# A new task order for the first chunk of an attention + softplus FFN kernel, and ten start-up products in place of eight

## The chip, the cores and the metric

The kernel runs on one core of one Trainium2 chip. The metric is the device time of one execution in microseconds, as the median of several runs. The core has five engines that run side by side, each working through its own queue strictly in order: TensorE (PE, matrix products; its weight loads are shown apart as PEld), VectorE (DVE), ScalarE (ACT), GpSimd (POOL), and SyncE (SP), which here only issues transfers between HBM and the on-chip memory. An instruction that has to wait holds up everything behind it in its own queue.

## The reference, cut to what matters

```python
# q, k, v: (8 batches, 8 heads, 576 positions, 64)
scores = scale * np.matmul(q, k.transpose(0, 1, 3, 2))
# heads 0-3: only the last 32 positions; heads 4-7: every 32nd position back
scores = np.where(masks[None, :, :, :], scores, -1000000000.0)
scores = scores - np.max(scores, axis=-1, keepdims=True)
attn = np.exp(scores)
attn = attn / (np.sum(attn, axis=-1, keepdims=True) + 1e-09)
x = np.matmul(attn, v)          # then laid out as (4608 tokens, 512)
h = x @ w_in                    # 512 -> 2048
g = np.maximum(h, 0.0) + np.log1p(np.exp(-np.abs(h)))
out = g @ w_out                 # 2048 -> 512
```

The weights arrive as float64 and all products are made from a high and a low part, so that the result keeps float32 accuracy: each of `x @ w_in` and `g @ w_out` is three products (high·high, high·low, low·high).

## The kernel before

**Tiling.** The 4608 tokens are cut into 9 chunks of 512. The hidden width of 2048 is cut into 16 slices `f` of 128. For each chunk and slice, `hidden` (L638) makes 12 products of 128x128 by 128x512 on TensorE (task `F`), `log_part` runs three activations on ScalarE (`A`, `Ae`, `Al`), `softplus` one VectorE instruction (`u`, L669), `g_high` and `g_low` split g into two parts (`Gh`, L264; `Gl`, L681), and `output` makes 12 more products (`O`, L688). Attention is done for pairs of heads, 4 pairs `n` per batch, 32 in all: `scores` (`S`), row maxima and exponentials (`X`, `Y`, `x`, `E`, `Z`), `guard` (`r`, L439), `reciprocals` (`R`, L443) and `normalize` (`M`, L447), transposes of the probabilities (`T` and `C` on TensorE for batch 0, `P` on VectorE after it, L457), `weighted` (`V`), and `x_part`, which writes the high and low part of x (`H`, L563; `L`, L561). `x` is the small instruction that scales the maxima for the exponentials (`bias_of`, L393).

**The first chunk.** Before and during chunk 0 the 16 slices of each weight matrix are loaded (`wi`, `wo`) and taken apart once: `a` on ScalarE (L589), `B`, `d`, `c` on VectorE (L593, L602, L619), then the high part `h` (L264) and the low part `l` (L634) on whichever of ScalarE, GpSimd and VectorE the lists below name. Chunk 0 also needs attention for batch 0 (pairs 0 to 3), and batch 1 (pairs 4 to 7) is done in the same stretch. In task names the digits after the letter are pair and half (`S31`), or the slice (`li7`).

**What sets the order.** For chunk 0 nothing is planned by the code: `FIRST` (L36) is a written-out list of 582 task names, and the loop at L945 emits them in just that sequence. Every engine's queue is the part of this list that belongs to it, and so is SP's queue of loads. Three more lists move single tasks to another engine than their usual one: `ON_POOL` (L63), `ON_VECTOR` (L66) and `ON_SCALAR` (L70). Behind `FIRST`, a `Plan` with costs and due times orders chunks 1 to 8; it is the same before and after.

**What limits how early a task may run,** beside its inputs: PSUM for hidden slices has two buffers (`ph`), so a slice waits for the `u` of an earlier one; `u` has two buffers, g three of each part, and the weight parts in work share four (`io`). The keys of a pair from n = 4 on lie in one of two buffers (`kT`), the raw queries in one of two halves of `prob`. The first thing on TensorE is the task `W`: `dummies` (L708) makes products of zeros into a buffer that nobody reads.

Of the kernel before, what the change touches and what calls it, by code (L numbers as in the profile page):

```python
# [33 lines left out]


FIRST = """  # L36
q0 D00 k0 W mask D01 S01 q1 X01 x01 D11 q2 D10 S00 X00 Y00 E01 D20 E00 Z00 r0 D21 R0 M0 k1 S10 X10
S11 wi2 ai2 X11 Y11 E11 T00 wi4 k2 S20 ai4 Bi2 x10 E10 di2 k3 ci2 Bi4 Z11 hi2 di4 r1 ci4 T01 C01
C00 q3 D30 D31 T02 X20 R1 Y20 M1 v0 V00 C02 H00 wi1 E20 ai1 S21 X21 L00 Z20 T10 wi0 li2 x21 T11
hi4 Bi1 di1 ci1 E21 r2 V01 H01 L01 C11 wo0 S31 C10 R2 v1 hi1 S30 X30 wo14 li4 wo1 T12 Y30 ai0 X31  # L40
M2 V10 H10 L10 T21 k4 C12 Bi0 v2 wi3 x31 E30 di0 Z30 V11 C21 E31 H11 T20 C20 li1 L11 ao1 T22 r3 R3
M3 V20 T32 ao0 ci0 C22 Bo0 H20 L20 C32 hi0 ai3 T30 C30 do0 wo3 li0 T31 V21 v3 co0 C31 V31 H21 L21
ho0 V30 Bi3 di3 ao3 H30 Fa0 Bo3 ci3 hi3 H31 L30 wi10 q4 D4 L31 F0 lo0 A0 Fa1 do3 co3 li3 Ae0 ho3
Al0 Bo1 do1 u0 S40 X40 wo4 ao4 lo3 Bo4 wo2 ao2 x40 Bo2 Gh0 Gl0 wi8 ai8 wo9 wi6 Bi8 E40 F1 F3 A3
Ae3 do2 di8 ci8 hi8 Al3 co2 do4 co1 ho1 wo5 A1 Ae1 Al1 u3 li8 Gh3 O0 lo1 ho2 lo2 ai6 u1 wi5 ai5
S41 wi11 X41 x41 Gl3 Bi5 Gh1 Gl1 ai11 Bi11 Bi6 E41 F4 wo7 q5 D5 wi9 wi15 F2 A2 di5 O1 di11 Ae2 Al2
di6 ci5 r4 hi5 ci6 wi14 R4 wi12 ci11 hi11 k5 wi13 u2 Gh2 M4 S50 X50 F8 co4 x50 P4 Gl2 O2 li11 A4
Ae4 hi6 ho4 li5 li6 Al4 u4 E50 S51 X51 v4 V40 ai9 Bi9 di9 x51 A8 wo6 Ae8 Al8 wi7 k6 q6 lo4 wo11
ao5 Bo5 O3 ci9 ai7 Bi7 di7 u8 Gh4 Gl4 F5 H40 L40 E51 ci7 ai10 Bi10 r5 R5 F6 Gh8 do5 D6 S60 hi7
di10 Gl8 co5 M5 V41 ci10 A5 Ae5 Al5 u5 O4 li7 A6 Ae6 Al6 X60 x60 u6 ho5 P5 Gh5 Gl5 hi9 lo5 wo12  # L50
li9 F7 H41 hi10 ao7 li10 v5 O5 ao6 Bo6 do6 L41 co6 E60 S61 X61 Gh6 Gl6 A7 Ae7 Al7 x61 Bo7 k7 V50
u7 F9 ho6 lo6 O6 wo10 H50 L50 ai13 Bi13 wo8 ao8 E61 q7 V51 Bo8 D7 di13 do7 A9 Ae9 ci13 r6 R6 hi13
S70 do8 li13 F13 co8 H51 co7 M6 Al9 u9 Gh7 ao10 X70 x70 L51 ho8 Gl7 F10 P6 ho7 ai12 lo7 Gh9 Gl9
lo8 E70 Bi12 Bo10 O7 ao9 Bo9 do10 S71 v6 V60 do9 k9 O8 co9 ho9 A13 Ae13 Al13 u13 F11 di12 A10 Ae10
Al10 Gh13 X71 u10 ao11 Bo11 co10 ho10 lo9 lo10 Gh10 Gl10 x71 H60 L60 do11 ai14 Bi14 O9 A11 V61
ci12 di14 E71 r7 R7 O10 hi12 ai15 ci14 Ae11 li12 H61 L61 co11 hi14 M7 li14 wo15 Al11 u11 F12 P7
Gh11 Gl11 wo13 ao12 A12 Ae12 F14 ho11 lo11 Gl13 ao13 Al12 u12 Gh12 A14 Ae14 Bo12 do12 Gl12 co12
ho12 O11 Bi15 di15 lo12 ci15 ao15 Bo15 v7 V70 H70 L70 ao14 Bo14 Qa0 Al14 u14 O12 q8 D8 hi15 li15
Bo13 do13 co13 ho13 lo13 do14 co14 ho14 V71 H71 F15 A15 Ae15 L71 O13 Q0 Gh14 Gl14 lo14 O14 Al15
u15 Gh15 Gl15 Q1 v8 do15 co15 ho15 lo15 QA0 Qu0 QA1 O15 y0 Qh0 k8 Ob15 Ql0 y3 y2 Qu1 Qh1 Ql1 y1 q9  # L60
"""
# [57 lines left out]
def attention_softplus_ffn(  # L119
# [588 lines left out]
    def dummies(n):  # L708

        for _ in range(0 if taken else n):  # L710
            nc.tensor.matmul(idle, lhsT=warm[:, :P], rhs=warm, start=True, stop=True)
# [308 lines left out]
```

## Time and profile before

| | |
|---|---|
| median of 3 runs | 899.62 us (898.74 to 899.64) |
| the profiled execution, its own time | 898.62 us |
| span, first to last instruction | 896.8 us |
| granted TensorE clock | 0.999 |
| PE busy | 878.9 us, 98% |
| VectorE busy | 601.3 us, 67% |
| ScalarE busy | 446.8 us, 50% |
| GpSimd busy | 58.1 us, 6%, all of it in the first 139 us |

The profile lists for each engine how long it was busy, and the trace behind it lists every instruction with its start, its duration, and, in brackets, how long its engine stood idle ahead of it and which engine's instruction (or transfer) ended that idle time. Names as `w_i<-a_i` say which tile is written from which. Times count from the start of the span. A row of the form "a:b" gives, for a stretch of the span, its length and the busy time of each engine with the number of instructions.

### The profile page before, as it was taken

What the parts mean: (1) busy time and instruction counts of PE and PEld (TensorE: products, weight loads), DVE (VectorE), ACT (ScalarE), POOL (GpSimd) and SP (SyncE); (2) the same over time, 40 slices, a digit from 0 to 9 for tenths busy, and PEclk for the clock granted to TensorE, in tenths of its full rate; (3) what the DMA queues carried; (4) which work ended last, traced back from release to release, by engine and by line L of the source; (5) the groups of instructions that cost most, each with busy time, mean ns of one, the idle gap of its engine ahead of it and who ended that gap; (6) DMA issues with size and microseconds to landing.
All of it is one profiled execution on the core that took longest, in us unless ns stands there. A gap on an engine that the chain in (4) does not pass through costs nothing.

```text
span 896.8 us, 14347 instructions
## 1 busy us (share of the span) xinstructions
PE 878.9 (98%) x5632; PEld 722.0 (81%) x5632; DVE 601.3 (67%) x1313; ACT 446.8 (50%) x795; POOL 58.1 (6%) x81
## 2 busy tenths in 40 slices
PE   6899999999999999999999999999999999999998
PEld 4777777888888888888888888888888888888886
DVE  8999996877777677666766676776776333333332
ACT  7998765445444545544544444454443343333332
POOL 6244330000000000000000000000000000000000
PEclk9999999999999999999999999999999999999999
DMA  9882212112211112111211121111200010001001
GB/s 339 297 303 92 86 37 88 44 57 60 76 43 45 44 44 89 32 44 45 91 44 44 42 76 31 44 45 44 91 18 18 1 48 1 0 1 48 1 1 47
DMA packets 50083, 58.27 MB, mean 65 GB/s; under 512 B 3168, under 2 KB 35296, under 8 KB 50016
## 3 DMA queue, kind: packets, MB, share of 16 engines
q1 hardware_dynamic: 49728, 57.03, 19.5%
q8 instruction: 44, 0.72, 0.3%
q10 hardware_dynamic: 288, 0.33, 0.1%
q14 instruction: 23, 0.19, 0.1%
HBM read 47.91 MB, written 9.44 MB: 64 GB/s over the span
## 4 chain that ended last, share of the span: by engine, by line
PE 87%; DVE 8%; ACT 2%; issue 1%; POOL 1%; DMA 0%; SPq 0%; DVEq 0%; POOLq 0%; ACTq 0%
PE py L688 41%; PE ph L648 40%; PE ps L355 2%; PE pv L525 2%; DVE pt L457 2%; PE po L525 1%; PE po L355 1%; DVE a_i L602 1%; DVE a_i L619 1%; DVE a_i L593 1%; DVE u L669 1%; DVE a_o L602 1%; DVE st L389 1%; DVE a_o L619 0%; DMA kT<-in_qk_dram 0%
## 5 line engine op out<-in xcount | busy, mean ns | idle before, releaser
L688 PE MATMUL py<-w_o,gh 128*128 128x512 f32 x1152 | 359.2, 393 | 0.3 <-POOL w_o L634 0.2
L648 PE MATMUL ph<-x_h,w_i 128*128 128x512 f32 x1152 | 356.4, 391 | 1.3 <-DVE w_i L634 0.9
L660 ACT ACTIVATE u<-ph 128x512 f32<-128x512 f32 x144 | 86.2, 599 | 396.8 <-PE ph L648 394.7
L648 PEld LDWEIGHTS ph<-x_h,w_i 128*128 128x128 f32 x1152 | 215.6, 188 | 47.2 <-DVE w_i L634 1.2
L688 PEld LDWEIGHTS py<-w_o,gh 128*128 128x128 f32 x1152 | 214.1, 188 | 47.7 <-POOL w_o L634 1.1
L648 PE MATMUL ph<-x_l,w_i 128*128 128x512 f32 x576 | 224.4, 390 | 0.0
L688 PE MATMUL py<-w_o,gl 128*128 128x512 f32 x576 | 224.4, 390 | 0.0
L669 DVE SCALAR_TENSOR_TENSOR u<-ph,u 128x512 f32<-128x512 f32 x144 | 99.2, 689 | 169.5 <-ACT u L665 167.9
L457 DVE STREAM_TRANSPOSE pt<-prob 32x192 f32<-32x192 f32 x448 | 137.1, 314 | 6.4
L688 PEld LDWEIGHTS py<-w_o,gl 128*128 128x128 f32 x576 | 108.2, 188 | 22.6
L648 PEld LDWEIGHTS ph<-x_l,w_i 128*128 128x128 f32 x576 | 108.2, 188 | 22.5
L681 DVE TENSOR_TENSOR gl<-u,gh 128x512 fp32r<-128x512 f32 x137 | 94.8, 692 | 12.0 <-POOL gh L264 0.8
L663 ACT ACTIVATE u<-u 128x512 f32<-128x512 f32 x144 | 91.2, 633 | 4.5
L665 ACT ACTIVATE u<-u 128x512 f32<-128x512 f32 x144 | 91.0, 632 | 4.3
L264 ACT COPY qT<-prob 64x576 f32<-64x576 f32 x56 | 70.6, 1261 | 2.3 <-DMA prob<-in_qk_dram 1.9
L264 DVE CAST gh<-u 128x512 fp32r<-128x512 f32 x130 | 55.7, 428 | 10.6 <-DVE u L669 0.5
L416 DVE TENSOR_TENSOR prob<-ps,mask_b 128x384 f32<-128x384 f32 x24 | 13.4, 558 | 50.2 <-PE ps L355 50.2
L355 PEld LDWEIGHTS ps<-kT,qT 128*64 128x64 f32 x720 | 24.0, 138 | 9.6 <-issue 8.1
L355 PE MATMUL ps<-kT,qT 128*64 128x64 f32 x720 | 27.6, 225 | 0.9 <-DMA kT<-in_qk_dram 0.9
L525 PE MATMUL pv<-pt,v_in 128*64 128x96 f32 x396 | 22.1, 248 | 1.0 <-PE ps L355 1.0
L447 DVE TENSOR_TENSOR prob<-prob,st 128x576 f32<-128x576 f32 x27 | 21.6, 799 | 0.9
L416 DVE TENSOR_TENSOR prob<-po,mask_b 128x192 f32<-128x192 f32 x24 | 8.6, 357 | 19.3 <-ACT x_h L563 19.3
(101 smaller groups left out, 511.9 us busy)
## 6 DMA issues: line engine op xcount, KB each, us to landing
v_in<-in_v_dram SPq DMA_DIRECT2D x28, 320.0 KB, 3.5
out_dram<-o SPq DMA_DIRECT2D x35, 256.0 KB, 2.1
ri<-in_moe_w_in_dram SPq DMA_DIRECT2D x16, 512.0 KB, 8.0
ro<-in_moe_w_out_dram SPq DMA_DIRECT2D x16, 512.0 KB, 6.9
kT<-in_qk_dram SPq DMA_DIRECT2D x28, 288.0 KB, 2.9
prob<-in_qk_dram SPq DMA_DIRECT2D x28, 288.0 KB, 2.7
v_in<-in_v_dram SPq DMA_DIRECT2D x28, 48.0 KB, 2.7
room<-in_v_dram SPq DMA_DIRECT2D x4, 320.0 KB, 6.8
```

The costliest lines, as they stand in the source:

```text
L264: (engine.copy if engine is nc.scalar else engine.tensor_copy)(dst, src)
L355: nc.tensor.matmul(ps[rows[place], 64 * (x - lo) : 64 * (x - lo) + 64], lhsT=blocks_of(n)[:, c // 32].rearrange("p h l -> p (h l)"), rhs=k ...
L416: nc.vector.tensor_tensor(pv, sv, m, op=ALU.add)
L457: nc.vector.transpose(pt[32 * (i + c) : 32 * (i + c) + 32, h, a : a + hi - lo, 32 * i : 32 * i + 32,], src[:, lo:hi, 32 * c : 32 * c + 32],)
L525: nc.tensor.matmul(po[64 * h : 64 * h + 64, TILE * x : TILE * x + TILE], lhsT=vs[n][:, a, h, :], rhs=pt_of(n, a)[:, h, a % 2], start=True, ...
L648: nc.tensor.matmul(ph, lhsT=w32["i", f][:, half, cc * P : (cc + 1) * P], rhs=x_of(x, cc)[:, t0 : t0 + n], start=(i == 0), stop=(i == 3 * N ...
L660: nc.scalar.activation(us[c, f], phs[c, f], AF.Abs)
L663: nc.scalar.activation(u, u, AF.Exp, scale=-1.0)
L665: nc.scalar.activation(u, u, AF.Ln, bias=1.0)
L669: nc.vector.scalar_tensor_tensor(u, in0=phs.pop((c, f)), scalar=0.0, in1=u, op0=ALU.max, op1=ALU.add)
L681: engine.tensor_tensor(g, us.pop((c, f)), ghs[c, f].bitcast(F32), op=ALU.subtract)
L688: nc.tensor.matmul(py[t], lhsT=g[:, sl], rhs=w32["o", f][:, half], start=(f == 0 and n == 0), stop=(f == NFC - 1 and n == 2),)
```

## The change

`FIRST` is replaced by another sequence of the same 582 tasks; `ON_POOL`, `ON_VECTOR` and `ON_SCALAR` name other tasks; and `W` makes ten products in place of eight. Nothing else differs; the tables take one line more, so every line number below them is one higher afterwards.

```diff
 FIRST = """
-q0 D00 k0 W mask D01 S01 q1 X01 x01 D11 q2 D10 S00 X00 Y00 E01 D20 E00 Z00 r0 D21 R0 M0 k1 S10 X10
...
+W mask q0 D00 k0 D01 S00 X00 Y00 q1 D11 S01 X01 E00 x01 Z00 k1 D10 S11 X11 q2 D20 Y11 E01 r0 wi0
...
 ON_POOL = """
-x01 D10 D20 hi2 D30 hi0 hi3 ho1 x50 hi6 Gh8 x60 hi13 x70 ho9 Gh13 x71 ho11 hi15 ho14 Gh15 ho15
+D10 D20 x10 D31 hi0 x21 r2 x31 r3 hi3 hi1 ho1 Gh0 ho2 x41 hi4 r4 x50 x51 x60 Gh6 x61 r6 ho8 ho10
+ho9 x71 r7 hi14 hi15 ho13 ho14 ho15
 ON_VECTOR = """
-D00 M1 C21 M3 li0 lo0 li3 Gl0 li8 Gh3 lo1 Gl3 Gl1 lo4 Gl8 M5 Gl6 li13 lo9 lo10 Gl10 li12 M7 Gl12
-lo12 li15 lo13 Gh14 Gl14 lo14 Gl15 lo15
+D01 M0 C00 M3 li3 li1 li2 lo1 Gl0 li9 lo2 li4 Gl1 Gl4 li6 lo6 Gl6 lo7 Gl7 li12 lo8 M6 Gl9 lo11
+li14 M7 lo13 Gl14 Gl15
 ON_SCALAR = """
-y3
+y1 y3
...
-    first["W"] = lambda: dummies(8)
+    first["W"] = lambda: dummies(10)
```

Counted over the lists, VectorE has 13 instructions fewer, GpSimd 12 more and ScalarE one more. Of the tasks that a list places, these change in number: `r` on GpSimd 0 to 5, `x` on GpSimd 5 to 9, `ho` on GpSimd 5 to 8 (ScalarE 11 to 8), `lo` on GpSimd 7 to 9 (VectorE 9 to 7), `li` on GpSimd 10 to 8 (VectorE 6 to 8), `Gl` on GpSimd 7 to 8 (VectorE 9 to 8), `Gh` on ScalarE 11 to 14 (VectorE 2 to 0, GpSimd 3 to 2). `M` keeps its four on each engine, but M0 and M1 change places.

Three places show how rows move. The first is VectorE's queue early in pair 0's softmax (`st_0` and `early_l0` belong to pair 0, `st_1` and `early_l2` to pair 1; the `a_i` are input weights in work). Before:

```order
L439 TENSOR_SCALAR st_0_175<-st_0_175 128x9
L443 RECIPROCAL st_0_175<-st_0_175 128x9
L389 TENSOR_REDUCE st_1_223<-py2_106 128x6
L389 TENSOR_REDUCE st_1_223<-py3_107 128x3
L376 TENSOR_TENSOR early_l2_93<-py3_107,st_1_223 128x3x64
L593 TENSOR_SCALAR a_i_2_235<-a_i_2_235 128x512
L393 TENSOR_SCALAR st_1_223<-st_1_223 128x6
L602 SCALAR_TENSOR_TENSOR a_i_2_235<-ri_2_233,a_i_2_235 128x512
```

The same place afterwards:

```order
L440 TENSOR_SCALAR st_0_181<-st_0_181 128x9
L390 TENSOR_REDUCE st_1_209<-py2_106 128x6
L444 RECIPROCAL st_0_181<-st_0_181 128x9
L448 TENSOR_TENSOR early_l0_91<-early_l0_91,st_0_181 128x9x64
L594 TENSOR_SCALAR a_i_0_247<-a_i_0_247 128x512
L603 SCALAR_TENSOR_TENSOR a_i_0_247<-ri_0_219,a_i_0_247 128x512
L620 SCALAR_TENSOR_TENSOR a_i_0_247<-ri_0_219,a_i_0_247 128x512
L390 TENSOR_REDUCE st_2_279<-py1_105 128x3
```

`normalize` of pair 0 (the row that writes `early_l0`) now stands in VectorE's queue, a maximum of pair 1 fills the place between `guard` and the reciprocal, and the first weights taken apart are slice 0, not slice 2.

The second place is GpSimd's queue behind its start-up fills, from its first copy of a raw query on. Before:

```order
L264 COPY early_h2_92<-raw_q1_173 64x18x32
L264 COPY early_h1_94<-raw_q2_179 64x18x32
L447 TENSOR_TENSOR early_l0_91<-early_l0_91,st_0_175 128x9x64
L264 CAST w_i_2_283<-a_i_2_235 128x512
L264 COPY early_h3_96<-raw_q3_301 64x18x32
L634 TENSOR_TENSOR w_i_2_283<-a_i_2_235,w_i_2_283 128x512
L634 TENSOR_TENSOR w_i_4_376<-a_i_4_268,w_i_4_376 128x512
L447 TENSOR_TENSOR early_l1_95<-early_l1_95,st_2_316 128x9x64
L634 TENSOR_TENSOR w_i_1_409<-a_i_1_336,w_i_1_409 128x512
```

Afterwards:

```order
L265 COPY early_h1_94<-raw_q2_211 64x18x32
L394 TENSOR_SCALAR st_1_209<-st_1_209 128x6
L265 COPY early_h3_96<-raw_q3_251 64x32x18
L265 CAST w_i_0_281<-a_i_0_247 128x512
L394 TENSOR_SCALAR st_2_279<-st_2_279 128x3
L448 TENSOR_TENSOR early_l2_93<-early_l2_93,st_1_209 128x9x64
L635 TENSOR_TENSOR w_i_0_281<-a_i_0_247,w_i_0_281 128x512
L440 TENSOR_SCALAR st_2_279<-st_2_279 128x9
L394 TENSOR_SCALAR st_3_355<-st_3_355 128x3
L448 TENSOR_TENSOR early_l1_95<-early_l1_95,st_2_279 128x9x64
L635 TENSOR_TENSOR w_o_0_437<-a_o_0_297,w_o_0_437 128x512
```

The small instructions of `bias_of` and `guard` stand here now, between the long ones; of long two-input rows in this piece there are four where there were five.

The third place is SP's queue at the end of chunk 0 (`kT_0` and `kT_1` hold the keys of even and odd pairs, `prob` raw queries, `out_0_dram` the result). Before:

```order
L293 DMA v_in_102<-in_v_dram 96x128
L300 DMA v_in_102<-in_v_dram 128x5x128
L704 DMA out_0_dram<-o_0_0_1778 128x512
L282 DMA kT_0_100<-in_qk_dram 128x576
L704 DMA out_0_dram<-o_0_3_1792 128x512
L704 DMA out_0_dram<-o_0_2_1795 128x512
L704 DMA out_0_dram<-o_0_1_1803 128x512
```

Afterwards the load of `kT_0` for pair 8 stands some fifteen places further up, right behind that of pair 7:

```order
L576 DMA ro_9_1230<-in_moe_w_out_dram 128x512
L283 DMA kT_1_101<-in_qk_dram 128x576
L283 DMA kT_0_100<-in_qk_dram 128x576
L570 DMA ri_13_1324<-in_moe_w_in_dram 128x4x128
L570 DMA ri_15_1333<-in_moe_w_in_dram 128x4x128
L576 DMA ro_10_1339<-in_moe_w_out_dram 128x512
```

The load of pair 8's keys no longer stands behind the first result's transfer.

More of the change, by code (lines that the diff above doesn't have):

```diff
@@ L36 @@
 FIRST = """
-q0 D00 k0 W mask D01 S01 q1 X01 x01 D11 q2 D10 S00 X00 Y00 E01 D20 E00 Z00 r0 D21 R0 M0 k1 S10 X10
[L38 to L59, printed above, removed]
@@ L60 @@
-u15 Gh15 Gl15 Q1 v8 do15 co15 ho15 lo15 QA0 Qu0 QA1 O15 y0 Qh0 k8 Ob15 Ql0 y3 y2 Qu1 Qh1 Ql1 y1 q9
+W mask q0 D00 k0 D01 S00 X00 Y00 q1 D11 S01 X01 E00 x01 Z00 k1 D10 S11 X11 q2 D20 Y11 E01 r0 wi0
+S10 X10 D21 x10 k2 S21 ai0 wo0 q3 D31 S20 R0 M0 E10 Bi0 di0 ci0 X21 hi0 E11 T00 x21 C00 ao0 Z11 r1
+X20 T01 C01 Bo0 D30 v0 R1 do0 V00 H00 T02 C02 L00 Y20 co0 M1 k3 S31 X31 E21 E20 Z20 V01 li0 wi1
+S30 H01 L01 ai1 Bi1 r2 di1 x31 R2 M2 wi3 ai3 T10 C10 T11 C11 v1 T12 ho0 lo0 Bi3 V10 T21 X30 Y30
+di3 C12 H10 L10 V11 E30 T20 E31 Z30 C21 ci3 H11 v2 L11 r3 R3 M3 C20 ci1 T22 wi2 ai2 Bi2 V20 C22
@@ new lines @@
+H20 L20 di2 hi3 li3 T32 k4 wo1 C32 wi9 T31 ao1 T30 C31 v3 C30 hi1 li1 V21 H21 wo2 ao2 L21 V31 wi4
+V30 ci2 Bo1 Bo2 ai9 H31 L31 Fa0 q4 H30 L30 F0 wi10 do1 co1 Bi9 di9 wo3 Fa1 hi2 li2 D4 S40 ci9 A0
+Ae0 Al0 ho1 lo1 ao3 F1 u0 Gh0 X40 x40 F2 Bo3 Gl0 ai4 Bi4 hi9 li9 di4 do2 co2 ho2 v4 A1 ci4 E40 S41
+X41 x41 wi5 ai5 q5 Bi5 Ae1 Al1 u1 wo15 D5 lo2 O0 wi6 hi4 di5 li4 F3 Gh1 Gl1 O1 ci5 A2 Ae2 wi8 ai8
+do3 co3 ai10 k5 E41 S50 r4 hi5 wo12 Bi8 li5 Al2 A3 di8 u2 R4 Ae3 M4 Al3 wi7 ai7 ci8 wi12 hi8 X50
+x50 F4 u3 Gh3 Bi10 di10 ci10 F5 Gh2 Gl2 wo5 wo4 ho3 lo3 E50 P4 O2 A4 Gl3 q6 hi10 ao5 Bo5 Ae4 Al4
@@ new lines @@
+u4 wi11 S51 A5 Ae5 li8 X51 li10 ai6 Al5 Bi7 di7 V40 ci7 H40 x51 Gh4 Gl4 E51 r5 F8 hi7 do5 u5 ao4
+L40 O3 D6 Bi6 A8 Ae8 Al8 wi14 V41 H41 Bo4 li7 di6 do4 co4 ho4 ci6 hi6 R5 M5 k6 wo6 lo4 co5 Gh5 S60
+u8 Gh8 X60 F7 ao6 ho5 x60 E60 Gl5 li6 F6 A6 O4 ai11 L41 P5 wo7 ao7 wo8 Gl8 A7 Bo6 do6 Bo7 Ae6 Al6
+v5 V50 H50 S61 Ae7 Al7 lo5 O5 co6 ho6 u6 Gh6 Bi11 L50 do7 X61 x61 ai12 Bi12 F9 lo6 q7 wo9 D7 Gl6
+V51 co7 di12 E61 di11 ci11 H51 L51 ho7 k7 S70 X70 ci12 u7 lo7 hi11 li11 r6 k8 A9 O6 ao9 Bo9 x70
+Gh7 Ae9 Gl7 ao8 F11 do9 Bo8 do8 co8 Al9 u9 wi13 ai13 Bi13 di13 hi12 li12 wi15 ho8 lo8 co9 wo10
@@ new lines @@
+ao10 Bo10 O7 R6 ci13 M6 A11 do10 hi13 F10 O8 co10 ho10 Ae11 Al11 Gh9 u11 Gh11 ho9 lo9 F12 Gl9 O9
+lo10 P6 wo11 A10 Ae10 Al10 u10 ao11 Bo11 ao12 E70 S71 ai15 do11 Bi15 v6 V60 q8 Gl11 A12 Ae12 co11
+li13 F13 Gh10 H60 X71 L60 ai14 Bo12 V61 k9 Gl10 wo14 di15 H61 Al12 do12 L61 u12 Bi14 co12 O10 wo13
+ho11 lo11 di14 ci14 ci15 A13 Ae13 Al13 u13 Qa0 x71 E71 r7 hi14 R7 O11 li14 Gh13 F14 ho12 lo12 Gh12
+Gl12 O12 Gl13 A14 Ae14 Al14 M7 P7 u14 hi15 li15 ao13 Bo13 ao14 do13 co13 ao15 v7 V70 ho13 H70 F15
+A15 L70 V71 H71 lo13 Bo14 do14 co14 ho14 lo14 O13 Ae15 L71 v8 Al15 u15 Gh15 Q1 Gh14 Gl14 O14 Bo15
@@ L61 @@
+do15 D8 Q0 QA1 co15 Gl15 Qu1 QA0 Qu0 ho15 lo15 O15 Qh0 y0 Ob15 q9 y1 Qh1 Ql0 y2 y3 Ql1
 """
 ON_POOL = """
-x01 D10 D20 hi2 D30 hi0 hi3 ho1 x50 hi6 Gh8 x60 hi13 x70 ho9 Gh13 x71 ho11 hi15 ho14 Gh15 ho15
+D10 D20 x10 D31 hi0 x21 r2 x31 r3 hi3 hi1 ho1 Gh0 ho2 x41 hi4 r4 x50 x51 x60 Gh6 x61 r6 ho8 ho10
+ho9 x71 r7 hi14 hi15 ho13 ho14 ho15
 """.split()
 ON_VECTOR = """
-D00 M1 C21 M3 li0 lo0 li3 Gl0 li8 Gh3 lo1 Gl3 Gl1 lo4 Gl8 M5 Gl6 li13 lo9 lo10 Gl10 li12 M7 Gl12
-lo12 li15 lo13 Gh14 Gl14 lo14 Gl15 lo15
+D01 M0 C00 M3 li3 li1 li2 lo1 Gl0 li9 lo2 li4 Gl1 Gl4 li6 lo6 Gl6 lo7 Gl7 li12 lo8 M6 Gl9 lo11
```

## The prediction

> **What bounds the kernel now.** I first cut the span where the work changes character: at the first product of a hidden slice, and at the end of chunk 0's products (columns: length of the stretch, then busy time of PE, PEld, DVE, ACT, POOL).
>
> ```profile
> 0.00:32.64 32.64, 22.04 (x480) 17.02 (x480) 28.24 (x60) 25.49 (x68) 18.40 (x42) 1.00 0.87 305
> 32.64:145.30 112.66, 110.13 (x678) 87.00 (x676) 106.75 (x224) 89.37 (x203) 39.67 (x39) 1.00 0.43 146
> 145.30:896.80 751.50, 746.74 (x4477) 618.01 (x4476) 466.31 (x1030) 331.98 (x525) 0.00 (x0) 1.00 0.14 42
> ```
>
> TensorE is idle for 10.6 us of the first stretch (32.64 - 22.04), for 2.5 of the second, 4.8 of the third. The third is the unchanged plan, with TensorE as its bound; whatever the first two stretches gain or lose goes through to the end. In the second stretch there is little left to win on TensorE itself: 2.5 us. But VectorE, with 106.75 of 112.66 us, is as full, so it can also take time away.
>
> Next the chain of waits at the end of that stretch, which tells who waits for whom.
>
> ```profile
> 112.70 1.77 DVE prob L447
> 114.47 0.61 DVE u L669
> ...
> 115.11 0.63 ACT gh L264
> ...
> 115.80 1.30 POOL gl L681
> 117.10 0.57 POOL w_o L264
> ...
> 117.74 1.30 POOL w_o L634
> ...
> 119.08 2.79 PE py L688 x11
> ...
> 142.00 0.48 ACT o L264
> 142.50 0.35 SPq L704
> ...
> 142.91 3.46 DMA kT<-in_qk_dram
> ```
>
> Up to 119 us the chain runs on VectorE, ScalarE and GpSimd and TensorE follows; from there TensorE runs closed up. It stops once more: the scores of pair 8 wait for their keys, whose load stood in SP's queue behind the first result (142.50). On TensorE's timeline:
>
> ```profile
> 32.00 0.72 PE L525 MATMUL pv<-early_l,room 128*64 128x96 f32 x12 [0.16 <-DVE x_l L561]
> 32.64 0.73 PE L648 MATMUL ph<-x_h,w_i 128*128 128x512 f32 x2
> ...
> 146.41 0.92 PE L355 MATMUL ps<-kT,qT 128*64 128x64 f32 x24 [0.94 <-DMA kT<-in_qk_dram]
> ```
>
> Just ahead of the first hidden product TensorE waits for VectorE again. And the second weight matrix's slice 13 shows how thin the margin is late in the chunk:
>
> ```profile
> 130.11 0.69 DVE L634 TENSOR_TENSOR w_o<-a_o,w_o 128x512 fp32r<-128x512 f32 x1 [0.69 <-ACT w_o L264]
> ...
> 131.01 0.62 PE L688 MATMUL py<-w_o,gh 128*128 128x512 f32 x2
> ```
>
> VectorE finishes its low part at 130.80, TensorE takes it up at 131.01. So **the bound is VectorE's queue**, read at such points, with TensorE right beside it.
>
> **The change, part by part.**
>
> *Two more products in W.*
>
> ```profile
> 1.18 3.59 PE L711 MATMUL idle<-room 128*128 128x512 bf16 x8 [1.18 <-DVE room L207]
> 5.39 0.57 PE L355 MATMUL py<-early_l,early_h 128*64 128x64 f32 x12 [0.62 <-ACT early_h L264]
> ```
>
> ```profile
> L711 PE MATMUL idle<-room 128*128 128x512 bf16 x8 | 3.6, 631 | 1.2 <-DVE room L207 1.2
> ```
>
> Eight take 3.59 us, of which the last one's own 0.63 us: one starts every (3.59 - 0.63)/7 = 0.42. Ten let the next product start at 1.18 + 10 x 0.42 = 5.4 us; the first scores start at 5.39 and wait for ScalarE. They fill a gap of 0.62 us: +0.05 at most, 0 to +0.85 if the copy of q comes earlier.
>
> *The way to the first hidden product.* Pair 0's first wait on VectorE:
>
> ```profile
> 6.08 0.36 DVE L389 TENSOR_REDUCE st<-py 128x3 f32<-128x192 f32 x1 [1.09 <-PE py L340]
> 6.94 0.56 DVE L389 TENSOR_REDUCE st<-py 128x6 f32<-128x384 f32 x1 [0.50 <-PE py L340]
> ...
> 8.76 0.56 DVE L385 TENSOR_REDUCE st<-early_l 128x6 f32<-128x384 f32 x1 [0.67 <-ACT early_l L381]
> ```
>
> ```profile
> 10.12 1.15 POOL L447 TENSOR_TENSOR early_l<-early_l,st 128x576 f32<-128x576 f32 x1 [0.44 <-ACT early_h L264]
> ```
>
> VectorE stands idle here for 2.3 us, with nothing else ready. The new order puts other pairs' maxima into these places and has VectorE normalize pair 0 itself, right behind the reciprocal. I followed the new queue by hand, as an estimate from such rows: scores of half 0 out at 6.8, maximum and subtraction to 8.0, ScalarE's wide exponential and then the three of half 1 to 9.6, `guard`, a maximum of pair 1 and the reciprocal to 10.6, the product to 11.3. GpSimd ended it at 11.27 before; so pair 0 gains nothing, but VectorE has done 0.7 us more work by then, that product. Between there and the last low part of x, which releases TensorE's row at 32.00, the queue differs by two `guard` and two `bias_of` less, one L619 less and one L634 more: about 0.6 us at the spacing of such rows. Together -1.3.
>
> This could be more. Three of VectorE's rows in that stretch were stretched by a GpSimd row beside them, one of them here:
>
> ```profile
> 18.88 1.28 POOL L634 TENSOR_TENSOR w_i<-a_i,w_i 128x512 fp32r<-128x512 f32 x1 [1.65 <-ACT w_i L264]
> ...
> 18.94 1.51 DVE L593 TENSOR_SCALAR a_i<-a_i 128x512 uint32<-128x512 uint32 x1
> ```
>
> An undisturbed L593 takes 0.42 (below), so this one cost 1.1 us. Walked on by hand with none of them, the new order normalizes pair 3 at 24.8, ends the transposes at 26.8 and the last low part of x at 28.5, and starts the first hidden product at 29.0 us, -3.6. With five long GpSimd rows there before and five after, I expect them again: bounds -3.6 and 0, taken -1.3.
>
> *VectorE's load up to slice 13 of w_out.* Counted in the two orders, ahead of that L634 there stand 5 L439, 4 L393, 2 L593, one L681 and one cast of g fewer, and 2 L634 more.
>
> ```profile
> L393 DVE TENSOR_SCALAR st<-st x7: 152/163/1270, 11.5 to 84.0; 128x3 f32<-128x3 f32 x5, 128x6 f32<-128x6 f32 x2
> ...
> L439 DVE TENSOR_SCALAR st<-st x9: 157/166/1240, 9.3 to 153.4; 128x9 f32<-128x9 f32 x9
> ```
>
> ```profile
> L593 DVE TENSOR_SCALAR a_o<-a_o 128x512 uint32<-128x512 uint32 x15 | 6.2, 422 | 0.0
> L681 DVE TENSOR_TENSOR gl<-u,gh 128x512 fp32r<-128x512 f32 x9 | 6.2, 684 | 0.8 <-POOL gh L264 0.8
> L634 DVE TENSOR_TENSOR w_o<-a_o,w_o 128x512 fp32r<-128x512 f32 x8 | 5.5, 685 | 0.8 <-ACT w_o L264 0.7
> L264 DVE CAST gh<-u 128x512 fp32r<-128x512 f32 x2 | 1.2, 578 | 0.0
> ```
>
> With medians and means: 5 x 0.166 + 4 x 0.163 + 2 x 0.42 + 0.68 + 0.58 - 2 x 0.69 = 2.2; neighbouring rows overlap by some 0.08 us each, so I take 2.0. Of these 0.6 stand in the front already: **-1.4** for the second stretch. What is late next is TensorE, idle there for only 2.5.
>
> *More on GpSimd.* Its 12 extra instructions are mostly short ones. Long two-input ones go from 28 to 29 (one `Gl` more; `li` and `lo` cancel).
>
> ```profile
> 10.00:136.00 126.00, 116.33 (x1030) 92.91 (x1026) 122.44 (x261) 104.31 (x252) 48.66 (x46) 1.00 0.53 183
> ```
>
> ```profile
> 13.77 1.71 POOL L264 COPY early_h<-raw_q 64x576 f32<-64x576 f32 x1
> 14.28 1.24 DVE L439 TENSOR_SCALAR st<-st 128x9 f32<-128x9 f32 x1
> ...
> 112.22 1.64 POOL L634 TENSOR_TENSOR w_i<-a_i,w_i 128x512 fp32r<-128x512 f32 x1 [7.64 <-ACT w_i L264]
> 112.62 1.85 DVE L447 TENSOR_TENSOR prob<-prob,st 128x576 f32<-128x576 f32 x1
> ```
>
> ```profile
> L681 POOL TENSOR_TENSOR gl<-u,gh 128x512 fp32r<-128x512 f32 x7 | 9.2, 1310 | 4.1 <-ACT gh L264 4.1
> L393 POOL TENSOR_SCALAR st<-st x5: 226/242/613, 7.1 to 104.3; 128x6 f32<-128x6 f32 x3, 128x3 f32<-128x3 f32 x2
> ```
>
> From the first to the last of these pairs there are eight, each stretched by about 1.1 us: 8.8 us for 48.7 us of GpSimd's work. GpSimd's own extra, from 3 casts more for `ho` (0.57 each, in the chain above), one less for `Gh`, one L681 (1.3), four `x` (0.24) and five `r` (between 0.24 and 0.61, the nearest row's), is 4.6 to 6.5 us, so some 5.6. At the share 8.8/48.7 that would be +1.0; by long rows, 1 x 8.8/29, +0.3. Every stretched row stands beside a long one, so I take +0.4, with bounds 0 and +5.6.
>
> The Trainium skill, in "GPSIMD Engine Reference", section "8. Key points", says that GpSimd shares its on-chip memory interfaces with VectorE and contends with VectorE instructions in a two-port mode or with two inputs from that memory. The stretched rows above agree in kind (L593 and L439 have one such input, L447 two). Taken to the letter it would charge VectorE with all of GpSimd's extra time, +5.6 in place of +0.4; the trace charges 18%.
>
> *Pair 8's keys.* Their load moves ahead of the first result, to behind pair 7's keys: the 0.94 us wait goes, **-0.95**, 0 if something else is late there. All four first results now go through ScalarE, 0.48 us each in the chain above; the hidden slice between them and their buffers' next use covers that.
>
> The sum: -1.3 - 1.4 + 0.4 - 0.95 + 0.05 = **-3.2**. The profiled execution took 898.62 us, 1.0 below the median of the runs, 899.62; so 895.4 against itself, **896.4** as a median.
>
> **The rivals.**
>
> *TensorE sets the middle after all* (no gain but the keys). If the front's gain only lets TensorE run into a later wait (the new order gives pair 5's transposes and slice 11's GpSimd low part as little room as the old one had), -0.95 and at most a few tenths are left: 898.6. For it: 110.13 busy of 112.66. Chance 0.23.
>
> *The front gains all of it.* No stretched rows, first hidden product at 29.0: -3.6 - 1.4 + 0.4 - 0.95 + 0.05 = -5.5, 894.1. Against it: as many long GpSimd rows stand there as before. Chance 0.20.
>
> *GpSimd charges VectorE* (slower). All 5.6 us of its extra time show up in VectorE's queue between 32.64 and 136 us, the front's better filling is lost the same way, and only the 2.0 of removed work and the keys remain: +5.6 - 2.0 - 0.95 = +2.6, 902.2. It decides from the point where about two thirds of GpSimd's extra time is paid. For it: eight stretched rows. Against it: most of GpSimd's rows stretch nothing. This is the page's rule at its strictest. Chance 0.15.
>
> **How the numbers follow.** The forecast (894.8 to 898) has 0.42. Faster by over 0.2% (1.8 us, about what a measurement of this kernel can tell from no change) means below 897.8: the forecast and the larger gain, 0.62. Within it: 0.23. Slower: 0.15. The range has 893.0 below, a little past the larger gain, and 901.0 above, between no change and the full price of GpSimd; about 0.05 lies under it and 0.12 over it.
>
> **What would show each step.** The first hidden product (L649 afterwards) at 31.3 us, between 29 and 32.6: the front. VectorE's last low part of w_out's slice 13 near 128.5 instead of 130.8: its load. No wait for kT near 143: the keys. Stretched VectorE rows beside long GpSimd rows: eight or nine; twelve or more would be the slower rival. W's ten products end by 5.7 and the first scores start by 5.5. I would be wrong if a new in-order wait opens between 32 and 136 us: TensorE's idle time there would pass 2.5 us, most likely behind the transposes of pair 5, or behind GpSimd's low parts of slices 8 and 11.

## The result and the profile after

| | before | after |
|---|---|---|
| runs, median (lowest to highest) | 899.63 us (898.74 to 899.64) | 892.44 us (891.77 to 893.00) |
| ratio after / before, 95% interval | | 0.9922 [0.9905, 0.9939] |
| profiled execution, time / span | 898.62 / 896.8 us | 891.98 / 890.2 us |
| first hidden product | 32.64 us | 29.65 us |
| scores of pair 8, the end of chunk 0's products | 146.41 us, after a wait of 0.94 | 139.74 us, no wait |
| VectorE rows stretched by 0.4 us or more beside a GpSimd row, 10 to 136 us | 8 | 3 |

The change makes the kernel 7.2 us faster in the medians, 6.6 us between the two profiled executions; the prediction was 3.2. All of the 6.6 lies ahead of the scores of pair 8 (146.41 - 139.74 = 6.67). Three executions of later variants, one each of six_memset, front_only and best_again, ran 1257 to 3122 us, and no ratio below counts them.

First the stretches of the prediction, now of the changed kernel (length, then busy time of PE, PEld, DVE, ACT, POOL):

```profile
0.00:29.65 29.65, 23.33 (x482) 18.15 (x482) 24.84 (x56) 24.05 (x66) 20.64 (x46) 1.00 0.94 317
29.65:139.65 110.00, 108.76 (x678) 87.49 (x676) 100.85 (x215) 90.40 (x206) 47.71 (x47) 1.00 0.45 157
139.65:890.20 750.55, 746.66 (x4477) 617.72 (x4476) 466.12 (x1030) 332.04 (x525) 0.00 (x0) 1.00 0.14 42
```

The front is 2.99 us shorter, the middle 2.66, and the third stretch 0.95, as much as the wait for the keys (0.94). VectorE was busy in 106.75 of the middle's 112.66 us and is now busy in 100.85 of 110.00, while TensorE is idle for 1.2: **TensorE is the bound of the middle now**. Its timeline at the points that the prediction showed:

```profile
29.01 0.72 PE L526 MATMUL pv<-early_l,room 128*64 128x96 f32 x12 [0.50 <-DVE x_l L562]
29.65 0.73 PE L649 MATMUL ph<-x_h,w_i 128*128 128x512 f32 x2
...
60.03 0.73 PE L649 MATMUL ph<-x_h,w_i 128*128 128x512 f32 x2 [1.06 <-DVE u L670]
...
139.74 0.92 PE L356 MATMUL ps<-kT,qT 128*64 128x64 f32 x24
```

The row at 60.03 is the one wait over 0.3 us that is left between the first hidden product and pair 8's scores. The chain of waits, which before ran on VectorE, ScalarE and GpSimd up to 119 us, now goes over to TensorE at that point and stays there:

```profile
57.40 0.59 ACT u L661
58.00 0.57 DVE a_o L594
58.57 0.73 issue
59.30 0.69 DVE u L670
...
60.03 3.01 PE ph L649 x12
63.05 2.72 PE py L689 x12
```

The "issue" of 0.73 us stands inside a VectorE row. That row, with what GpSimd and VectorE did around it (start, length, engine):

```profile
54.04 1.29 POOL L635 TENSOR_TENSOR w_o<-a_o,w_o 128x512 fp32r<-128x512 f32 x1
55.29 1.31 POOL L682 TENSOR_TENSOR gl<-u,gh 128x512 fp32r<-128x512 f32 x1
56.54 2.55 POOL L635 TENSOR_TENSOR w_i<-a_i,w_i 128x512 fp32r<-128x512 f32 x2
```

```profile
54.97 2.98 DVE L458 STREAM_TRANSPOSE pt<-prob 32x96 f32<-32x96 f32 x9
57.98 1.40 DVE L594 TENSOR_SCALAR a_o<-a_o 128x512 uint32<-128x512 uint32 x1
59.30 0.68 DVE L670 SCALAR_TENSOR_TENSOR u<-ph,u 128x512 f32<-128x512 f32 x1
```

GpSimd's long rows run closed up, one every 1.25 us, beside VectorE's transposes and keep their length. Then the shift L594 starts and is held until the last of them ends, at 59.09: 1.40 us in place of 0.42. Where GpSimd's row starts second, it is the one that gets longer, here 1.74 us in place of some 1.3:

```profile
17.31 0.81 DVE L620 SCALAR_TENSOR_TENSOR a_o<-ro,a_o 128x512 uint32<-128x512 uint32 x1
...
17.53 1.74 POOL L635 TENSOR_TENSOR w_i<-a_i,w_i 128x512 fp32r<-128x512 f32 x1
```

Of the eight stretched rows of the kernel before, 8.3 us together, three are left, 2.0 us together: the shift above and two more.

```profile
85.69 1.19 DVE L635 TENSOR_TENSOR w_o<-a_o,w_o 128x512 fp32r<-128x512 f32 x1
...
106.41 0.89 DVE L594 TENSOR_SCALAR a_o<-a_o 128x512 uint32<-128x512 uint32 x1
```

A second profile of the changed kernel (after_again) has four, 2.8 us together. Yet GpSimd has as many long rows as before (30, from 29) and is busy for more of that time (59.79 us of 126, from 48.66). So the question for the experiments: are the stretched rows that vanished the 3.4 us by which the prediction fell short?

### The profile page after: what moved, and what is told of

It is laid out like the page before. It is cut to its first block, busy times and chain, and to the rows that moved or that the text cites. A ratio compares the mean times of both kernels' runs of the same rounds, so it can differ in the third digit from the quotient of the medians.

```text
span 890.2 us, 14364 instructions
## 1 busy us (share of the span) xinstructions
PE 878.7 (99%) x5634; PEld 723.4 (81%) x5634; DVE 591.8 (66%) x1300; ACT 446.5 (50%) x796; POOL 68.3 (8%) x93
## 4 chain that ended last, share of the span: by engine, by line
PE 93%; ACT 3%; DMA 2%; SPq 1%; issue 1%; DVE 0%; ACTq 0%
PE py L689 44%; PE ph L649 42%; PE ps L356 3%; PE pv L526 2%; PE po L526 1%; PE po L356 1%; DMA ro<-in_moe_w_out_dram 1%; DMA early_l<-in_qk_dram 1%; ACT qT L265 1%; ACT prob L400 0%; ACT a_i L590 0%; ACT u L661 0%; SPq L294 0%; SPq L570 0%; SPq L301 0%
```

## The experiments

All are compared with the kernel before on the same chip (medians of 899.2 to 899.7 us there). "Changed" stands for the changed kernel.

### The price of a meeting, by itself

probe adds rows behind the changed kernel's last result (its time means nothing): VectorE rows of four kinds, first beside a closed row of GpSimd's two-input subtractions, then the same rows alone.

```diff
+        for beside in (True, False):
+            if beside:
+                for r in range(60):
+                    nc.gpsimd.tensor_tensor(tf[0], tf[1], tf[2], op=ALU.subtract)
...
+                nc.vector.tensor_scalar(t[3], t[3], 3, 0x7FFFFFFF, ...)
+                nc.vector.scalar_tensor_tensor(v[0], in0=py[0], scalar=0.0, in1=v[0], ...)
...
+                nc.vector.tensor_tensor(v[1], v[1], v[0], op=ALU.subtract)
...
+                nc.vector.transpose(pt[0:32, 0, 0:6, 0:32], prob[0][0:32, 0:6, 0:32])
```

> The changed kernel with a stretch of rows added behind its last result, so its time is not compared. Twice the same rows on VectorE, first beside GpSimd rows of two inputs in a closed row, then alone: L594's shift (one SBUF input) in turn with L670's maximum (PSUM and SBUF), a two-input subtraction from SBUF in turn with that maximum, that maximum alone, and 32x32 transposes. Theory A: beside GpSimd the shift and the subtraction take their own time plus up to 1.3 us, one GpSimd row's length; the maximum from PSUM and the transposes take what they take alone. Rival (a shared memory port): all of them are some ten per cent longer, none by a whole row.

The groups of VectorE's rows beside GpSimd (busy time, mean ns), and then alone:

```profile
L961 DVE TENSOR_SCALAR probe<-probe 128x512 uint32<-128x512 uint32 x12 | 10.8, 902 | 2.9 <-ACT probe L953 2.9
L964 DVE SCALAR_TENSOR_TENSOR probe<-py,probe 128x512 f32<-128x512 f32 x12 | 8.1, 678 | 0.0
...
L968 DVE TENSOR_TENSOR probe<-probe,probe 128x512 f32<-128x512 f32 x12 | 11.1, 922 | 0.4
...
L977 DVE STREAM_TRANSPOSE pt<-prob 32x192 f32<-32x192 f32 x24 | 8.8, 366 | 0.8
```

```profile
L977 DVE STREAM_TRANSPOSE pt<-prob 32x192 f32<-32x192 f32 x24 | 8.8, 366 | 0.8
L968 DVE TENSOR_TENSOR probe<-probe,probe 128x512 f32<-128x512 f32 x12 | 8.3, 691 | 0.4
...
L964 DVE SCALAR_TENSOR_TENSOR probe<-py,probe 128x512 f32<-128x512 f32 x12 | 8.2, 687 | 0.0
L961 DVE TENSOR_SCALAR probe<-probe 128x512 uint32<-128x512 uint32 x12 | 5.0, 420 | 0.0
```

The shift goes from 420 to 902 ns and the subtraction from 691 to 922. The maximum that reads PSUM takes 678 beside GpSimd and 687 alone; twelve of them in a row take 8.67 us both times, and 24 transposes 9.56 us both times. So of the four kinds two wait and two are free. GpSimd waits too: its rows have a median of 1.26 us beside the maxima alone and beside the transposes, 1.33 beside the shifts and 1.59 beside the subtractions. The price is a wait for the end of the GpSimd row and not a slower rate: after the first rows the two engines fell into step, one GpSimd row to each pair of VectorE rows, so the wait was 0.46 us for most shifts, while rows that start at any time paid up to 1.1 in the kernel before. A wait of a whole GpSimd row, the theory's 1.3, was not seen. The Trainium skill, in "SBUF — State Buffer", section "Who interferes with whom", says that the ports which the two share are an exclusive lock: whoever issues first holds it for a whole instruction. The trace agrees: the shift that began at 57.98 us, inside a GpSimd row, was held until that row's end at 59.09, and the GpSimd row that began at 17.53, inside a VectorE row, took 1.74.

### The stretched rows taken out of the kernel before

eight_to_vector gives VectorE the eight pieces that GpSimd ran beside the stretched rows:

```diff
-x01 D10 D20 hi2 D30 hi0 hi3 ho1 x50 ...
+x01 D10 D20 hi2 hi0 hi3 ho1 x50 ...
...
+D30 li4 li1 Gl4 li7 lo6 M6 li14
```

> The kernel before with the eight GpSimd pieces that stand beside its eight stretched VectorE rows given to VectorE (D30, li4, li1, Gl4, li7, lo6, M6, li14). VectorE gets some 5.8 us more of its own work. Theory A (the stretch is a wait for the GpSimd row beside it): the 8.2 us of stretch go unless new pairs meet, so the time falls by 1 to 3 us. Rival (the stretch has another cause, or VectorE's work is what counts): the rows stay long or the work adds up, +2 to +5 us.

897.00 us, ratio 0.9975 [0.9966, 0.9984]: 2.5 us faster with some 5.8 us more of work on the engine that was full. One stretched row is left (1.25 us, an L440 at 15.19). The gain rests on the ten runs and not on the profile, whose execution was the slowest of them (898.58 us):

```profile
0.00:34.35 34.35, 25.25 (x480) 20.35 (x480) 27.93 (x63) 25.46 (x68) 14.08 (x39) 0.95 0.84 290
34.35:145.40 111.05, 109.47 (x678) 87.17 (x676) 104.26 (x229) 89.18 (x203) 32.52 (x34) 1.00 0.43 148
```

There the middle is 1.6 us shorter than before and the front 1.7 longer. In that front the granted clock (the third figure from the end, 0.95 on average) stood at 0.5 from 20.73 to 24.14 us; whether this or the pieces moved to VectorE made it longer is open.

six_memset leaves VectorE's work alone and shortens six of GpSimd's rows instead; the low parts named are not computed.

```diff
+        if (w, f) in (("i", 4), ("i", 1), ("i", 7), ("o", 6), ("i", 14)):
+            part.pop((w, f))
+            nc.gpsimd.memset(t[:, 1].bitcast(F32), 0.0)
+            return
...
+        if (c, f) == (0, 4):
+            us.pop((c, f))
+            nc.gpsimd.memset(g.bitcast(F32), 0.0)
+            return
```

> The kernel before, with six of the eight GpSimd rows that stand beside its stretched VectorE rows left out: the low parts of w_in's slices 1, 4, 7 and 14, of w_out's slice 6 and of g's slice 4 are not computed, GpSimd fills them with zeros instead. VectorE's own work stays as it was. Theory A (the stretch is a wait for the GpSimd row): those six rows fall to their own time, 6.2 us in all, unless others meet, and the time falls by 2 to 4 us, more than the eight pieces on VectorE gave, which added 5.8 us to it. Rival (VectorE's stretched rows don't set the time): within 0.5 us of the kernel before.

895.23 us, ratio 0.9955 [0.9939, 0.9971]: 4.0 us faster, the upper end of theory A. Its stretches:

```profile
0.00:31.64 31.64, 24.26 (x480) 19.36 (x480) 26.18 (x60) 25.33 (x68) 16.82 (x42) 0.95 0.90 314
31.64:141.11 109.47, 109.05 (x678) 87.42 (x676) 102.84 (x224) 89.16 (x203) 36.01 (x39) 1.00 0.44 151
```

The middle falls from 112.66 to 109.47 us with the same 224 VectorE rows, and TensorE is idle in it for 0.4. What remains open here: the zeros (0.52 us) are also ready sooner than a low part (1.3 us), so not all of the 3.2 must come from VectorE; but in the middle of the kernel before TensorE waited for a low part of GpSimd's for only 0.2 us. eight_to_vector has no such help.

front_only does this for the front's three stretched rows alone; pair 1's `guard` goes to GpSimd, and the middle is left as it was.

```diff
-x01 D10 D20 hi2 D30 hi0 ...
+x01 D10 D20 hi2 D30 r1 hi0 ...
...
+        if (w, f) in (("i", 4), ("i", 1)):
+            part.pop((w, f))
+            nc.gpsimd.memset(t[:, 1].bitcast(F32), 0.0)
+            return
```

> The kernel before with its three stretched VectorE rows of the front taken away and nothing done to the middle: the low parts of w_in's slices 4 and 1 are not computed (GpSimd fills them with zeros), and pair 1's guard (r1, L439) goes to GpSimd. Theory A (the three rows are the front's 3.0 us): VectorE's rows up to the first hidden product shrink by about 3.0 us and the first hidden product comes at 29.6 to 30.2 instead of 32.64, a little later where TensorE's first scores run slow; the time falls by 2 to 3 us. Rival (the front is set by VectorE's order, by the loads or by ScalarE): first hidden product at 31.5 or later, less than 1.2 us.

897.65 us, ratio 0.9980 [0.9970, 0.9989], 1.7 us: between the two theories. front_only_2 is the same kernel, run again for its profile.

> front_only once more, for its profile. Theory A: first hidden product at 29.6 to 30.2, and the middle 1 us longer than before. Rival: first hidden product at 30.9 or later, the middle as before.

897.27 us, ratio 0.9975 [0.9961, 0.9989]; its stretches up to pair 8's scores:

```profile
0.00:31.08 31.08, 23.39 (x480) 18.62 (x480) 25.48 (x59) 25.32 (x68) 17.42 (x43) 0.95 0.93 321
31.08:144.74 113.66, 110.41 (x678) 86.96 (x676) 106.73 (x224) 90.14 (x205) 39.33 (x39) 1.00 0.43 148
```

VectorE's busy time up to the first hidden product falls by 2.76 us (28.24 to 25.48), as theory A had it, but that product comes only 1.56 us earlier: VectorE now stands idle for 5.60 us of the front (31.08 - 25.48) in place of 4.40. Of these 1.2 us, 0.75 are two waits that the kernel before does not have:

```profile
17.22 0.36 DVE L389 TENSOR_REDUCE st<-py 128x3 f32<-128x192 f32 x1 [0.36 <-PE py L355]
17.97 0.46 DVE L561 TENSOR_TENSOR x_l<-pv,x_h 128x288 fp32r<-128x288 f32 x1 [0.39 <-ACT x_h L563]
```

They follow a stretch in which this execution's granted clock was halved, while in the kernel before it read 1.00 all through the front:

```profile
11.30:14.71 3.41, 3.35 (x58) 3.27 (x60) 3.34 (x8) 2.51 (x14) 1.40 (x4) 0.50 1.09 372
```

The 24 scores that began at 12.59 us took 1.49 us in place of 0.92, and those that VectorE awaits at 17.22 began at 16.64 in place of 15.87. So this front does not settle the matter. The three rows are worth 1.56 us in it, and up to 1.56 + 0.75 = 2.3 without these two waits, an estimate; the rival's product time is the one that came, but in a front that a slower clock had held up. By the run time they are worth 1.7 and 2.5 us in the two measurements, on both sides of theory A's lower bound. What the front gains the middle keeps: from 32.64 or 31.08 to the scores of pair 8, less their own wait (0.94 and 0.82 us), it is 112.83 and 112.84 us.

### Order and choice of engines apart

old_tables takes the new `FIRST` with the old `ON_POOL`, `ON_VECTOR` and `ON_SCALAR`; new_tables the old `FIRST` with the new ones. The edit is that of the change, one half each.

> The new order with the old choice of engines (GpSimd, VectorE and ScalarE do what they did before). Theory A (collisions): VectorE gets 2.0 us of work back; beyond that the time follows the stretched VectorE rows between 10 and 136 us, each some 1.1 us. With two of them as in the changed kernel 893 to 894.5; with eight as in the kernel before 896 to 899. Rival B (VectorE's amount of work decides, not how its rows meet GpSimd's): 893 to 894.5 whatever the number of stretched rows. Rival C (the order only matters together with its engines): slower than the kernel before, over 900.

> The old order with the new choice of engines. Theory A (collisions): 2.0 us less on VectorE and the rest by the stretched rows: with eight or more 897 to 899, with two 892 to 894. Rival B (amount of work alone): 897 to 898 whatever their number. Rival C (an order fits one choice of engines): GpSimd's rows come late for TensorE, over 900.

936.65 us (ratio 1.0409 [1.0390, 1.0428]) and 914.02 us (1.0165 [1.0148, 1.0182]): rival C's times in both. 17 and 14 stretched VectorE rows between 10 and 136 us, more than in either whole kernel, at 42.95 and 49.03 us of GpSimd rows; so their number doesn't follow GpSimd's time. In old_tables the scores of pair 8 start at 184.83 us, 38.4 later than before. Its stretch up to them:

```profile
36.58:185.00 148.42, 126.92 (x683) 97.80 (x682) 120.06 (x224) 90.65 (x205) 45.81 (x41) 0.89 0.36 121
```

With the front, TensorE is idle for 20 us more than before and busy for 19 more, at a granted clock of 0.89 where it had 1.00. So about half of the loss is plain waiting for other engines, as the longest of TensorE's waits in old_tables, then in new_tables, show (us in total, times, longest); the other half is rows that took longer.

```profile
PE ph L648 <- DVE u L669: 6.7, 5, 3.1
PE ps L340 <- ACT prob L399: 4.8, 1, 4.8
PE py L688 <- DVE w_o L634: 3.1, 1, 3.1
```

```profile
PE py L341 <- DMA mask_b<-in_masks_dram: 3.7, 1, 3.7
PE ph L649 <- DVE u L670: 3.7, 6, 0.9
```

The reason that rival C gave for new_tables, GpSimd's rows late for TensorE, is not the main one: such waits are 1.5 us there. An order fits one choice of engines; which of the two halves removed the stretched rows can't be told apart, since neither half does it alone.

### The keys, the products of W and what is left

k8_early moves pair 8's keys ahead of pair 9's in the kernel before, k8_late puts them back behind the first result in the changed one; w8 makes eight products in the changed kernel.

```diff
-... S71 v6 V60 do9 k9 O8 ...
+... S71 v6 V60 do9 k8 k9 O8 ...
```

```diff
-... hi11 li11 r6 k8 A9 ... O15 Qh0 y0 Ob15 ...
+... hi11 li11 r6 A9 ... O15 Qh0 y0 k8 Ob15 ...
```

> The kernel before with the load of pair 8's keys moved ahead of pair 9's, nothing else. The wait of 0.94 us for kT goes and the time falls by 0.9 to 1.0 us against the kernel before. Rival: something else is late at pair 8's scores, 0 to -0.3 us.

> The changed kernel with the load of pair 8's keys put back behind the first result. If the keys are worth what the wait for kT took, the scores of pair 8 wait again by about 0.9 us and the time is 0.9 to 1.1 us above the changed kernel's. Rival: with the front and the middle shorter the load is hidden by other work or another wait is late there; then 0 to 0.3 us.

> The changed kernel with eight products in W instead of ten, nothing else. In the profile of the changed kernel the tenth product ends 0.28 us ahead of the first scores, which wait for ScalarE. If the first scores' start is set by that copy alone, eight products give the same time within 0.2 us. If the two products keep TensorE's clock up (the rival that the change's words suggest), the granted clock of the first 30 us falls and the time rises by 0.5 us or more.

k8_early: 899.12 us, ratio 0.9993 [0.9985, 1.0002], an interval that holds both theories. In its profile the wait is gone: the scores of pair 8 start at 145.60 us in place of 146.41, behind a first hidden product at 32.67 in place of 32.64. k8_late: 894.35 us, ratio 0.9936 [0.9922, 0.9949] against the changed kernel's 0.9922, +1.3 us with intervals that overlap; there the scores wait again, 0.71 us; their keys, issued at 138.67 us, take 3.1 to 3.2 to land, though the profile names a ScalarE row that ends at the same moment. Its profiled execution also had a later front (first hidden product at 31.04), so the +1.3 is not the keys alone. So the keys' price rests on the waits in the profiles, 0.94 and 0.71 us; the times are too coarse for it. w8: 892.99 us, ratio 0.9924 [0.9912, 0.9937], no difference that the runs can tell, and the granted clock reads 1.00 up to 30 us, so the rival does not show. The lead of the tenth product over the first scores, put at 0.28 us above, is 0.06 in the changed kernel's profile (5.63 to 5.69); with eight products the scores start at 5.57.

u4_first, front_fix, u4_k6 and best try to take out what waits are left in the changed kernel.

```diff
-... hi10 ao5 Bo5 Ae4 Al4 u4 wi11 ...
+... hi10 ao5 Ae4 Al4 u4 Bo5 wi11 ...
```

```diff
-... S01 X01 E00 x01 Z00 k1 D10 S11 ...
+... S01 X01 E00 Z00 k1 D10 x01 S11 ...
-ON_POOL: D10 D20 ...
+ON_POOL: D10 x01 D20 ...
```

```diff
-... Gl3 q6 hi10 ... R5 M5 k6 wo6 ...
+... Gl3 k6 q6 hi10 ... R5 M5 wo6 ...
```

The first is u4_first's edit, the second front_fix's; u4_k6 has the first and the third, best all three.

> The changed kernel with the shift of w_out's slice 5 (L594) moved behind slice 4's maximum (L670) in the written order. In the changed kernel's profile that shift was stretched to 1.40 us beside a GpSimd row, the L670 behind it came late and TensorE waited 1.1 us for it, the only wait over 0.3 us that is left before 140 us. If that wait is real lost time, the kernel gains 0.8 to 1.2 us on the changed one (about 891). Rival: the shift is late for something else, or TensorE waits for the next thing ScalarE or the loads bring: 0 to 0.3 us.

> The changed kernel with the bias of pair 0's second half (x01, L394) on GpSimd, behind its first copy of q (D10) and ahead of its second (D20). In the profiled run of the changed kernel D20 started at 8.93 us, after a wait for its load, and L394 took 0.17 us on VectorE; in two kernels with the same front D20 started at about 8.4, L394 took 1.0 to 1.2 us beside it and the first hidden product came 1.4 us later (31.0 in place of 29.65). Theory: this one collision is the spread of the changed kernel's runs (891.8 to 893.0); with it excluded by the order all runs lie at 891.7 to 892.3. Rival: GpSimd's own L394 (0.24 to 0.6 us) is later than VectorE's and the whole moves up, 892.5 or more, or the spread stays.

> As best, without the front's part: 1.0 us below the changed kernel in either kind of run, 890.7 to 892.1, if the two waits at 60 and 67 us are real lost time; else as the changed kernel, 891.8 to 893.0.

> As front_fix, and with w_out slice 5's shift behind slice 4's maximum as in u4_first, and the load of pair 6's keys (k6) ahead of pair 6's queries on SP's queue: in u4_first TensorE no longer waited at 60 us but 0.96 us at 67.55, for those keys, whose load stood behind the load of the queries that waits for a buffer until 59.3. If both waits are gone: about 1.0 us below front_fix, 890.7 to 891.2. Rival: something else is late by then: as front_fix, 891.7 or more.

u4_first, 892.83 us (0.9922 [0.9910, 0.9935]), gains nothing: the wait at 60 us is gone, and the next one opens at once.

```profile
67.55 0.92 PE L356 MATMUL ps<-kT,qT 128*64 128x64 f32 x24 [0.96 <-DMA kT<-in_qk_dram]
```

These keys were issued behind the queries of the same pair, which wait for their buffer. With both edits, u4_k6: 891.44 us (0.9911 [0.9896, 0.9926]); with all three, best: 891.41 us (0.9909 [0.9894, 0.9923]). front_fix alone: 892.13 us (0.9917 [0.9902, 0.9931]); its spread did not go (891.45 to 892.55); in its profile a later copy of q, whose load came at 12.7 us, met another VectorE row (L620, 1.57 us). The gains are near the limit of the measurement, so the changed kernel and best ran once more side by side.

> The changed kernel as it is. 891.8 to 893.0, in two groups about 1.1 us apart by whether VectorE's L394 at 8.4 us meets GpSimd's second copy of q; median 892.5.

> The variant best as it is, beside the changed kernel on the same chip: 0.9 to 1.3 us below it (890.5 to 892.0), if the waits at 60 and 67 us were lost time; level with it if the chip made the difference.

892.21 us (0.9923 [0.9910, 0.9937]) and 891.70 us (0.9913 [0.9900, 0.9927]). The two groups of runs that I expected of the changed kernel don't show (891.67, 892.00, 892.21, 892.48, 893.74). best is ahead both times, by about 0.1%, though the intervals overlap. What it gains is plain in the profiles: the middle of the changed kernel's second profile, then of best:

```profile
29.94:139.94 110.00, 108.86 (x679) 87.50 (x677) 100.85 (x215) 90.01 (x205) 47.68 (x47) 1.00 0.46 157
```

```profile
29.99:139.01 109.02, 109.02 (x678) 87.27 (x676) 100.20 (x215) 89.76 (x205) 47.66 (x47) 1.00 0.46 159
```

In best TensorE shows no idle time between the first hidden product and the scores of pair 8; by that measure only the front is left to win.

## Why the prediction was wrong

The direction, the place and the bound were right; the size was not: 3.2 us predicted, 6.6 measured between the profiled executions.

- **More on GpSimd: the step that failed.** It said that the stretched rows would recur, "eight or nine", and charged +0.4 for one more long GpSimd row. Three were left. The step took the price of GpSimd to follow the number of its long rows (8.8 us for 29). It follows which VectorE row starts beside which GpSimd row: 29, 30, 26 and 26 long rows made 8, 3, 17 and 14 stretched ones in before, after, old_tables and new_tables. A new order rolls these dice again, so "they recur" was no neutral assumption but one outcome; its bounds, 0 to +5.6, left out a gain altogether. Taking the stretch out of the old order is worth 4.0 us by itself (six_memset), more than the 3.4 that the prediction missed; how much of the change's gain each vanished row brings is not measured.
- **The way to the first hidden product:** -1.3 predicted, -3.0 measured. None of the front's three stretched rows recurred, so "I expect them again" is the words that missed, and the walk without them, -3.6, is the nearer number. VectorE's busy time in the front falls by 3.40 us (28.24 to 24.84): 2.97 are what the three rows had been stretched by, and 0.4 is left for the work removed, counted as 0.6. The 0.7 of filling doesn't show. VectorE's idle time rises from 4.40 to 4.81, its waits for pair 0, 2.26 us in three pieces before, are one of 2.18 ahead of the first maximum, and pair 0's product ends at 11.68 in place of the walk's 11.3. How much of the -3.0 the stretched rows bring by themselves is only bounded, by front_only_2's 1.56 to 2.3. The front also differs between executions: in two kernels with the changed kernel's front (k8_late, u4_first) the first hidden product came at 31.0, with VectorE's L394 at 8.4 and 8.6 us stretched to 1.20 and 1.01 us beside the copy D20; in the changed kernel's first profile that copy waited 0.55 us for its load and missed it.
- **VectorE's load in the middle:** -1.4 and the +0.4 predicted, -2.66 measured. VectorE is busy for 5.9 us less there: five stretched rows, 5.34 us, became three, 1.96; the other 2.5 is more than the 1.4 of removed work that was counted. Its low part of w_out's slice 13 ends at 124.38 us, where 128.5 had been named. The gain is cut off by TensorE, as "what is late next" said. But TensorE's idle time of 2.5 us was not the limit that I took it for: its busy time for the same 678 rows fell too, from 110.13 to 108.76 us. Part of that can be waiting counted as busy: a product shows as 0.39 us long and the next one starts 0.23 after it, so a delay of up to 0.16 leaves no idle time. six_memset shows that taking the stretch away is enough for this gain (-3.2 in the middle with all of VectorE's work in place), eight_to_vector that it counts even against more work; what the removed work alone would have brought was not run.
- **Pair 8's keys:** -0.95 predicted; the wait is gone, and the third stretch is 0.95 us shorter. Right.
- **Two more products:** +0.05 predicted. The ten end at 5.63, as said ("by 5.7"), the first scores start at 5.69 and not by 5.5; with eight products (w8) the time is the same as far as the runs can tell.
- **The rivals.** "The front gains all of it" (894.1) was nearest; its reason, no stretched rows, was the right one, but it kept the middle's. "TensorE sets the middle" describes the kernel after the change, not what the change was worth. "GpSimd charges VectorE" fell: GpSimd's time rose by 11.1 us, twice the 5.6 that was added up, and the stretch of VectorE's rows fell by 6.3. What speaks for it is only that GpSimd's own rows got longer, as in the one at 17.53 us: its casts for w_out have a mean of 0.77 us in place of 0.61, and its `x` of 0.40 in place of 0.33.

## What to carry to other kernels

When two engines can block each other, list the rows that met in the profile, price each by what it delayed, and treat the sum as something that a new order draws afresh, with none and twice as many both inside the range. Put the blocking engine's long rows beside rows that it can't block (here the transposes and the maximum that reads PSUM), where they cost nothing. An order and a choice of engines are one thing: half of such a change can cost more than the whole brings.
